# A spatial sum in three passes and a last stretch of queries in four chunks of 128, in a two-layer attention and gMLP kernel

## The chip, the cores and the metric

One core of one Trainium2 chip. The metric is device time in microseconds; the program is launched as a whole, and a time is the median of several executions. Executions of one kernel mostly agree within about 0.3%.

## The reference, cut to what matters

Two layers, each of an attention block A and a gated block B, over 2048 positions of 512 features. A has 32 query heads of 16 and one shared key and value head, so its softmax takes 32 x 2048 x 2048 exponentials a layer. B sums over positions, so it needs every position of its own layer before its last step.

```python
def _A_ref(x, wq, wk, wv, wo):            # S = 2048, D = 512, H = 32, Dh = 16, one k and v head
    scores = einsum('bhqd,bkd->bhqk', q, k) * Dh ** (-0.5)
    p = softmax(scores)
    o = einsum('bhqk,bkd->bhqd', p, v)
    return o.transpose(0, 2, 1, 3).reshape(B, S, H * Dh) @ wo

def _B_ref(x, w_in, w_sp, b_sp, w_out):   # F = 1792, Fh = 896
    z = gelu(x @ w_in)
    z1 = z[..., :Fh]
    z2 = layernorm(z[..., Fh:])
    g = einsum('ts,bsf->btf', w_sp, z2) + b_sp[None, :, None]     # the spatial sum
    return (z1 * g) @ w_out

x = A_x
for _ in range(2):                        # written out twice in the source
    x = x + _A_ref(layernorm(x), ...)
    x = x + _B_ref(layernorm(x), ...)
```

## The kernel before

The positions lie in 16 tiles of 128. Attention goes by chunks of queries; when a chunk is done its tiles go through the projection, the second layernorm, `w_in`, gelu and the norm of `z2`. The spatial sum over source tiles `s` goes in passes: tiles 0 to 7, tiles 8 to 13 (the early pass), and a closing that folds tiles 14 and 15 into the last step. `(8, 14, 4)` means tiles 8 to 13, once chunk 4 is through its gelu.

```python
self.chunks = [[256, 256, 512, 512, 256, 128, 128], [512, 512, 512, 256, 128, 128]]
self.passes = [[(0, 8, 2), (8, 14, 4)], [(0, 8, 1), (8, 14, 3)]]
self.gelus = [[(0, 1, 2), (3, 4), (5,), (6,)], [(0, 1), (2, 3), (4,), (5,)]]
self.s_fin = 14
...
def spatial(self, s0, s1, layer):
    acc = s0 > 0
    early = s1 == self.s_fin
    pr = PRE if early else PRP
    ...
    for tc in range(4):                       # 512 target positions each
        ... # load of the weights of this pass
        for f in range(NF):                   # 7 blocks of 128 features: 28 jobs a pass
            # one matmul of 512 columns per source tile, summed in PSUM
            ...
            def ev_fn(e, b, tc=tc, f=f):      # the eviction: one DVE add out of PSUM into gp
                dst = self.gp[:, tc, f, :]
                return e.tensor_tensor(dst, self.b32(b), dst if acc else self.bb[:, 512 * tc:512 * tc + 512], ALU.add)
            pl, (ev,) = sc.job(pieces, [dict(fn=ev_fn, ...)], deps, pr)
            if early:
                self.early_first.append(sc.first_op)
```

The exponentials are shared between ACT, which does most of them, and DVE, which makes a power of two by bit arithmetic. The DVE's share is decided by this rule, among others: while the first matmul of an early-pass job is ready and not placed, no DVE exponential starts.

```python
if EF and any(o.start is None and o.ready is not None and o.ready <= t for o in k.early_first):
    return None
```

The closing goes over eight groups of 256 target positions: matmuls of 256 columns over tiles 14 and 15, cast out of PSUM, add of `gp`, product with `z1`, then `w_out`.

```python
seq = [(i, f, s) for i, f in enumerate(fs) for s in range(s0, s1)]      # s0, s1 = s_fin, 16
...
ad = sc.op("dve", ... ALU.add ...)            # + gp, SBUF only
ev = sc.op("dve", ... ALU.mult ...)           # * z1, SBUF only
```

First, the order of the instructions on each engine is made ahead of the launch, by a list scheduler in the kernel's own Python. It reckons with durations of its own, of which two matter here. They decide only the plan: the order of the instructions and, with it, which of ACT and DVE takes some of the exponentials and casts.

```python
def d_psum(n):
    return n * 1.042e-3 + 0.066      # a DVE operation out of PSUM

def d_sb(n, rate):
    return n * rate + 0.066          # a DVE operation on SBUF
```

The scheduler, a list scheduler in the kernel's own Python that makes the order of the instructions ahead of the launch, fills some of PE's pauses with matmuls of a zero operand, which compute nothing. They show in the profile as busy PE time, on the line with `zero`.

The softmax here doesn't subtract the row's maximum and nothing guards it: scores larger than these inputs give would overflow.

Of the kernel before, what the change touches and what calls it, by code (L numbers as in the profile page):

```python
# [388 lines left out]
PRE = 1.6  # L389
PRP = 2.5  # L390
# [55 lines left out]
class Kern:  # L446
    def __init__(self, nc, A_x, A_wq, A_wk, A_wv, A_wo, B_x, B_w_in, B_w_sp, B_b_sp, B_w_out, out):
# [9 lines left out]
        self.chunks = [[256, 256, 512, 512, 256, 128, 128], [512, 512, 512, 256, 128, 128]]  # L457
        self.passes = [[(0, 8, 2), (8, 14, 4)], [(0, 8, 1), (8, 14, 3)]]
        self.gelus = [[(0, 1, 2), (3, 4), (5,), (6,)], [(0, 1), (2, 3), (4,), (5,)]]
        self.s_fin = 14  # L460
# [193 lines left out]
    def ln(self, tiles, deps_t, dst, dst_deps, pr, urgent=False, on_pe=False):  # L654
# [48 lines left out]
        return [ev]  # L703
# [149 lines left out]
    def finish_group(self, g, pv_last):  # L853
# [37 lines left out]
        if g.fin:  # L891
            tr = self.transpose(self.oTt[:, par, :].rearrange("p (i r) -> p i r", i=4), self.oT[:, par, :],
                                [ev, self.rd_read[par]], f"oq{par}", 0.5)
            self.oT_read[par] = tr
            m = sc.op("dve", lambda e: rc(e, None), 0.18, [tr], 0.6)
            for h in hs:
                m = sc.op("dve", lambda e, h=h: nm(h, e, None), d_psum(256 // len(hs)), [m] + onr, 0.5)
                self.norms.append(m)
            self.rd_read[par] = m
            if g.v == 1 and g.q.s0 + g.q.ns == 4:  # L900
                norms = self.norms
                self.norms = []
                self.project(g, norms)
            return
# [16 lines left out]
    def project(self, g, norms):  # L921
# [7 lines left out]
        for h in range((nq + 1) // 2):  # L929
# [16 lines left out]
            if g.fin > 1:  # L946
                for qt in qts:
                    o = self.transpose(self.onT[:, qt, :, :], self.on[:, qt, :], norms + list(self.onT_read), f"ot{qt}", 0.7)
                    self.on_read[qt] = [o]
                    evs.append(o)  # L950
                continue
# [6 lines left out]
            evs.append(ev)  # L958
# [18 lines left out]
    def mixer_chunk(self, g):  # L977
# [9 lines left out]
        for i in range(0, nt, 2):  # L987
            ts = T[i:i + 2]
            evs += self.ln(ts, lambda t: [self.x_op[t]], self.xnTB[:, i:i + len(ts), :, :], war, pr, last, g.fin == 1)
# [32 lines left out]
        elif g.ci == batch[-1] and len(batch) > 1 and g.ci > self.passes[g.layer][0][2]:  # L1022
# [44 lines left out]
    def mix_rest(self, g, last, pr, batch):  # L1067
# [27 lines left out]
        for ci, (zt, zn, v) in zip(batch, zs):  # L1095
# [8 lines left out]
            elif ci == batch[-1] and len(batch) > 1 and ci > self.passes[g.layer][0][2]:  # L1104
# [39 lines left out]
    early_first = []  # L1144
    gp_read = {}


    def spatial(self, s0, s1, layer):
# [3 lines left out]
        early = s1 == self.s_fin  # L1152
        pr = PRE if early else PRP
        z2f = self.z2n[:].rearrange("p t f -> p (t f)")
        wsl = self.wsT[:].rearrange("p s t -> p (s t)")
        if early:

            nf = self.NT - s1
            parts = [(z2f[:, 4096:4096 + 512 * nst], range(4, 4 + -(-(512 * (nst + 1)) // FH))), (wsl[:, 0:512 * nst], None)]
            self.held_f = range(0, 5)  # L1160
# [7 lines left out]
        for tc in range(4):  # L1168
            if early:
                w_, held = parts[tc % 2]  # L1170
                w_ = w_.rearrange("p (s t) -> p s t", s=nst)
                war = self.last_ws[0] if held is None else [o for t in held for o in self.z2_read[t]]
                ld = self.dma(lambda e, w_=w_, tc=tc: e.dma_start(w_, self.ws_dv[:, s0:s1, 512 * tc:512 * (tc + 1)]),
                              war + self.ws_st[s0:s1], f"wsp{tc % 2}", nst * 131072, 1.0)
# [14 lines left out]
            for f in range(NF):  # L1189
# [16 lines left out]
                def ev_fn(e, b, tc=tc, f=f):  # L1206
                    dst = self.gp[:, tc, f, :]
                    return e.tensor_tensor(dst, self.b32(b), dst if acc else self.bb[:, 512 * tc:512 * tc + 512], ALU.add)  # L1208
                pl, (ev,) = sc.job(pieces, [dict(
                    fn=ev_fn, dur=d_psum(512), prio=max(1.0, pr - 1.5),  # L1210
                    deps=list(self.gp_read[(tc, f)]) + ([self.gp_ops[(tc, f)]] if acc else []))], deps, pr)
                if early:
                    self.early_first.append(sc.first_op)
# [5 lines left out]
            if not early:  # L1219
                for i in (0, 1) if nsl == 1 else (sl,):  # L1220
                    self.last_ws[i] = [users[-1]]
            elif held is None:
                self.last_ws[0] = [users[-1]]


    def closing(self, layer):
# [6 lines left out]
        self.hT_read = [[o for o in self.dx_s.end], [o for o in self.dx_s.end]]  # L1233
        z1r = self.z1s[:].rearrange("p (k f t) -> p k f t", k=2, f=NF)
        zl = [list(self.z1s_free), list(self.z1s_free)]
        for tc in range(8):
            tg, to = tc // 2, 256 * (tc % 2)
# [630 lines left out]
```

## Time and profile before

| | before |
|---|---|
| time, median of 2 runs (range) | 1796.28 us (1794.82 to 1797.75) |
| last exponential of layer 0 | 851.2 us |
| gap to the first exponential of layer 1 | 37.0 us |
| exponentials of layer 1 | 850.6 us |
| tail from the last exponential to the end | 58.0 us |

Between the first and last exponential of a layer, ACT sets the pace. The gap and the tail have no exponentials, and there the closing and the keys of the next layer (or the output) set it. So a change can move four numbers: two long stretches and two short ones.

The next lines are busy times by stretch of the kernel before. The columns are the stretch in us, its length, then busy us (and instructions) of PE, PEld, DVE, ACT and POOL, then the granted clock, the DMA share and GB/s. The first two are the last 60 us of exponentials in each layer, then come the gap and the tail.

```profile
791.20:851.20 60.00, 58.57 (x419) 17.98 (x426) 22.21 (x36) 59.66 (x53) 0.81 (x2) 1.00 0.15 45
1678.80:1738.80 60.00, 58.68 (x419) 17.50 (x425) 28.35 (x43) 59.54 (x53) 0.81 (x2) 1.00 0.14 45
...
851.20:888.20 37.00, 36.08 (x258) 20.25 (x262) 33.10 (x88) 20.05 (x37) 4.31 (x8) 1.00 0.30 77
1738.80:1796.80 58.00, 56.39 (x346) 30.76 (x350) 46.69 (x112) 22.72 (x40) 1.91 (x4) 1.00 0.37 108
```

Read the third column of busy time (DVE) in the first two lines: 22 and 28 of 60 us. That is the idle time that the change is after. Then read the first (PE) in the last two: 36.1 of 37.0 and 56.4 of 58.0. PE is packed where the closing runs.

What PE does in the first 17 us of the tail is in its timeline (start, length, line, operands, count):

```profile
1740.66 0.39 PE L866 MATMUL ps_all<-ident,oT 128*128 128x128 bf16 x4
1740.89 1.03 PE L1196 MATMUL ps_all<-z2n 128*128 128x512 bf16 x4
1741.87 0.40 PE L937 MATMUL ps_all<-ident,on 128*128 128x128 bf16 x4
1742.11 1.03 PE L1196 MATMUL ps_all<-z2n 128*128 128x512 bf16 x4
1742.97 1.03 PE L966 MATMUL ps_all<-wo_r,onT 128*128 128x512 bf16 x4
1743.83 0.59 PE L1196 MATMUL ps_all<-z2n 128*128 128x512 bf16 x2
1744.27 3.18 PE L1196 MATMUL ps_all<-wsT,z2n 128*128 128x512 bf16 x13
...
1751.68 5.13 PE L1196 MATMUL ps_all<-wsT,z2n 128*128 128x512 bf16 x23
```

Lines 866, 937 and 966 are the chain of the last tile (transpose, transpose, projection). Each waits for another engine. Between them lie left-over jobs of the early pass (1196), which had been ready for long.

### The profile page before, as it was taken

Reading aid. Unit: us, or ns where it says so; the run is one execution under the profiler, and the core shown is the slowest. Engines: PE = TensorE matmul, PEld = TensorE weight load, DVE = VectorE, ACT = ScalarE, POOL = GpSimd, SP = SyncE. Lnnn points to the kernel's source line nnn. Section 1 sums busy time; section 2 is a strip of 40 time slices with the busy share of each in tenths; the row PEclk is TensorE's granted clock in tenths of the full one; section 3 lists DMA queues with packets and bytes.
Section 4 is the critical chain, followed back from the end, with each engine's and each line's share of the span. In section 5 each row is a group of like instructions: output and inputs, shape, how many; then the busy total and the mean of one; then the engine's idle time right before and its main releaser. Section 6 shows DMA issues by size and latency. Waiting matters only on the chain.

```text
span 1796.8 us, 29474 instructions
## 1 busy us (share of the span) xinstructions
PE 1563.1 (87%) x11691; PEld 464.7 (26%) x11773; DVE 1655.7 (92%) x2488; ACT 1722.0 (96%) x1557; POOL 56.4 (3%) x99
## 2 busy tenths in 40 slices
PE   8888888888989888999988888888888898898999
PEld 4222222212222222223532222222222222222235
DVE  8999999999999999973999999999999999999748
ACT  8999999999999999999689999999999999999983
POOL 1000000000000000000110000000000100000000
PEclk9999999999999999999999999999999999999999
DMA  4535100011010110311310001000110111203123
GB/s 148 124 77 135 54 18 4 7 30 24 10 47 27 30 48 13 77 37 54 87 36 10 4 7 19 18 7 4 30 24 13 45 30 30 51 7 77 35 82 114
DMA packets 155465, 76.14 MB, mean 42 GB/s; under 512 B 108480, under 2 KB 152128, under 8 KB 155328
## 3 DMA queue, kind: packets, MB, share of 16 engines
q1 hardware_dynamic: 153744, 74.08, 16.2%
q8 instruction: 94, 1.54, 0.4%
q14 instruction: 43, 0.35, 0.1%
q10 hardware_dynamic: 1584, 0.16, 0.1%
HBM read 31.49 MB, written 17.83 MB: 27 GB/s over the span
## 4 chain that ended last, share of the span: by engine, by line
ACT 50%; issue 20%; PE 18%; DVE 11%; POOL 1%; DMA 0%; ACTq 0%; DVEq 0%
ACT Pa L1471 49%; PE ps_all L1815 5%; PE ps_all L1196 5%; PE ps_all L1558 3%; DVE E L1667 1%; DVE st L1124 1%; PE ps_all L1286 1%; DVE st L660 1%; PE ps_all L1796 1%; DVE Pd L1698 1%; PE ps_all L998 1%; PE ps_all L1037 1%; DVE X L1291 1%; DVE E L1694 1%; DVE E L1268 1%
## 5 line engine op out<-in xcount | busy, mean ns | idle before, releaser
L1471 ACT ACTIVATE Pa<-ps_all 128x1536 bf16<-128x1536 f32 (+1 forms) x1424 | 1612.3, 1454 | 12.7 <-PE ps_all L1815 11.0
L1815 PE MATMUL ps_all<-qs,kT 32*128 32x512 bf16 x4096 | 561.0, 385 | 194.6 <-ACT Pa L1471 179.5
L1667 DVE TENSOR_SCALAR E<-ps_all 128x512 f32<-128x512 f32 x540 | 364.6, 682 | 28.4 <-PE ps_all L1815 25.7
L1796 PE MATMUL ps_all<-zero 128*128 128x512 bf16 x1065 | 331.2, 393 | 19.8 <-DVE mv L1126 6.2
L1815 PEld LDWEIGHTS ps_all<-qs,kT 32*128 32x128 bf16 x4096 | 138.6, 91 | 790.9 <-ACT Pa L1471 771.1
L1698 DVE SCALAR_TENSOR_TENSOR Pd<-E 128x1536 uint16<-128x1536 f32 x180 | 314.9, 1749 | 2.2
L1558 PE MATMUL ps_all<-Pa,V 128*32 128x512 bf16 x3556 | 316.5, 385 | 0.2 <-DVE oT L859 0.2
L1558 PE MATMUL ps_all<-Pd,V 128*32 128x512 bf16 x540 | 182.6, 385 | 0.0
L1696 DVE TENSOR_TENSOR E<-E 128x1536 f16<-128x1536 f16 x180 | 171.1, 951 | 2.2
L1694 DVE TENSOR_TENSOR E<-E 128x1536 f16<-128x1536 f16 x180 | 170.8, 949 | 2.4
L1692 DVE TENSOR_SCALAR E<-E 128x1536 f16<-128x1536 uint16 x180 | 171.2, 951 | 1.5
L1196 PE MATMUL ps_all<-wsT,z2n 128*128 128x512 bf16 x568 | 160.5, 382 | 9.2 <-issue 3.8
L1796 PEld LDWEIGHTS ps_all<-zero 128*128 128x128 bf16 x1065 | 81.4, 98 | 189.8 <-issue 129.8
L1695 DVE TENSOR_SCALAR E<-E 128x1536 f16<-128x1536 f16 x180 | 98.9, 550 | 1.0
L1558 PEld LDWEIGHTS ps_all<-Pa,V 128*32 128x32 bf16 x3556 | 62.0, 94 | 114.6 <-issue 108.5
L1208 DVE TENSOR_TENSOR gp<-ps_all,gp 128x512 f16<-128x512 f32 x56 | 38.4, 688 | 52.8 <-PE ps_all L1196 52.7
L1196 PEld LDWEIGHTS ps_all<-wsT,z2n 128*128 128x128 bf16 x616 | 44.0, 97 | 78.7 <-issue 43.7
L998 PE MATMUL ps_all<-w_in_r,xnTB 128*128 128x448 bf16 x256 | 63.5, 356 | 0.9 <-DVE z2n L1009 0.4
L1037 PE MATMUL ps_all<-xnTB,w_in_r 128*128 128x512 bf16 (+2 forms) x364 | 63.1, 299 | 0.6 <-DVE z2n L1009 0.3
L664 POOL TENSOR_SCALAR ve<-mv 128x2 f32<-128x2 f32 (+1 forms) x28 | 11.8, 421 | 1395.8 <-DVE mv L662 1395.7
L1265 ACT ACTIVATE E<-ps_all 128x512 f16<-128x512 f32 (+1 forms) x52 | 26.6, 538 | 29.3 <-PE ps_all L1253 28.6
L1286 PE MATMUL ps_all<-E 128*128 128x512 bf16 x214 | 52.6, 380 | 1.8 <-DVE kT L741 0.8
(87 smaller groups left out, 947.7 us busy)
## 6 DMA issues: line engine op xcount, KB each, us to landing
wsT_scratch<-gp SPq DMA_DIRECT2D x16, 512.0 KB, 3.6
wsT<-wsT_scratch SPq DMA_DIRECT2D x8, 1024.0 KB, 5.4
z1s<-z_scratch SPq DMA_DIRECT2D x16, 448.0 KB, 3.7
z_scratch<-z1s SPq DMA_DIRECT2D x4, 896.0 KB, 5.5
z2n<-wsT_scratch SPq DMA_DIRECT2D x4, 768.0 KB, 4.8
wsT<-wsT_scratch SPq DMA_DIRECT2D x4, 768.0 KB, 5.6
X<-in_A_x_dram SPq DMA_DIRECT2D x8, 256.0 KB, 5.8
z2n<-wsT_scratch SPq DMA_DIRECT2D x2, 1024.0 KB, 8.6
```

Of the source, the lines that this page charges most:

```text
L998: ins = e.matmul(self.b32(b)[:, 0:448], self.xnTB[:, i, kd, :], self.w_in_r[:, kd, FH + h * 448:FH + (h + 1) * 448], start=(kd == 0), stop ...
L1196: ins = e.matmul(self.b32(b), self.z2n[:, s, f * 128:(f + 1) * 128], w_[:, s - s0, :] if s - s0 < na or not spare else wsp[:, s - s0 - na, :],
L1471: return e.activation(k.Pa[:, base:base + n, :], k.b32(b0, n).rearrange("p (k q) -> p k q", k=n), ACTF.Exp, scale=SCALE)
L1558: ins = e.matmul(k.b32(u.grp.pvb)[32 * j:32 * j + 32, :], k.V[:, u.kt, :], b.slot, tile_position=(0, 32 * j), start=u.first, stop=u.last)
L1667: c = k.sc.op("dve", lambda e: e.tensor_scalar(k.ey[:, s, 512 * i:512 * (i + 1)], k.b32(j.bank.idx)[:, 0:512], E_LOG2, E_BIAS, op0=ALU.mul ...
L1692: o2 = sc.op("dve", lambda e: e.tensor_scalar(x, lo, E_X * 2.0 ** -16, E_X * E_A, op0=ALU.mult, op1=ALU.add), d_sb(n, 0.521e-3), self.ops ...
L1694: o3 = sc.op("dve", lambda e: e.tensor_tensor(w, x, x, ALU.mult), d_sb(n, 0.521e-3), [o2, self.wfree], pr)
L1695: o4 = sc.op("dve", lambda e: e.tensor_scalar(w, w, E_C, None, op0=ALU.add), d_sb(n, 0.26e-3), [o3], pr)
L1696: o5 = sc.op("dve", lambda e: e.tensor_tensor(w, w, x, ALU.mult), d_sb(n, 0.521e-3), [o4], pr)
L1698: o7 = sc.op("dve", lambda e: e.scalar_tensor_tensor(po.bitcast(U16), y, E_D, w, op0=ALU.add, op1=ALU.add), d_sb(n, 1.042e-3), [o5] + self ...
L1796: return e.matmul(k.b32(pvb if b is None else b.idx), k.zero[:], k.zero[:, None, :].to_broadcast([P, 4, P]), start=b is not None, stop=b i ...
L1815: return e.matmul(self.b32(bank), self.kT[32 * j:32 * j + 32, g.v, kt * 128:(kt + 1) * 128], self.qs[32 * j:32 * j + 32, g.q.slot, :], til ...
```

## The change

The intent: keep the early pass from holding up DVE's exponentials any longer, and let it come earlier, so that DVE takes more of them. For that, the last 512 queries become four chunks of 128, the second pass covers tiles 8 to 12, a short third pass takes tiles 13 and 14 as soon as they are there, and the closing is left with tile 15 alone. With `EFB = 0` only the third pass stops DVE's exponentials. Four of seven of the third pass's evictions are an ACT copy and a DVE add on SBUF in place of a DVE add out of PSUM.

```diff
-        self.chunks = [[256, 256, 512, 512, 256, 128, 128], [512, 512, 512, 256, 128, 128]]
-        self.passes = [[(0, 8, 2), (8, 14, 4)], [(0, 8, 1), (8, 14, 3)]]
-        self.gelus = [[(0, 1, 2), (3, 4), (5,), (6,)], [(0, 1), (2, 3), (4,), (5,)]]
-        self.s_fin = 14
+        self.chunks = [[256, 256, 512, 512, 128, 128, 128, 128], [512, 512, 512, 128, 128, 128, 128]]
+        self.passes = [[(0, 8, 2), (8, 13, 4), (13, 15, 6)], [(0, 8, 1), (8, 13, 3), (13, 15, 5)]]
+        self.gelus = [[(0, 1, 2), (3, 4), (5, 6), (7,)], [(0, 1), (2, 3), (4, 5), (6,)]]
+        self.s_fin = 15
 ...
-        early = s1 == self.s_fin
-        pr = PRE if early else PRP
+        early = acc
+        fin = s1 == self.s_fin
+        pr = (PRC if fin else PRE) if early else PRP
 ...
+            if fin:
+                pr = 2.0 + 2 * CLS * tc - CL0
 ...
-                pl, (ev,) = sc.job(pieces, [dict(
-                    fn=ev_fn, ...
-                if early:
+                if fin and f % 7 in CST:                       # CST = (0, 2, 4, 6)
+                    pl, (ev,) = sc.job(pieces, [dict(
+                        fn=lambda e, b, st=st: e.activation(st, self.b32(b), ACTF.Copy), eng="act", ...
+                    ev = sc.op("dve", lambda e, st=st, dst=self.gp[:, tc, f, :]: e.tensor_tensor(dst, st, dst, ALU.add), ...
+                else:
+                    pl, (ev,) = sc.job(pieces, [dict(
+                        fn=ev_fn, ...
+                if fin or early and EFB:                       # EFB = 0
                     self.early_first.append(sc.first_op)
 ...
         for tc in range(8):
+            pr = 2.0 + CLS * tc                                # closing, CLS = 0.1
```

Cut: where the weights of each pass are held, the staging buffers' bookkeeping, and tile 13 using the same transposes as the other small chunks.

## The prediction

> **What bounds the kernel now.** I read first the busy shares, then the forty slices, then the costliest groups, then the stretches of each layer's end, then the DVE's waits there, then the timeline of the last 60 us.
>
> ```profile
> PE 1563.1 (87%) x11691; PEld 464.7 (26%) x11773; DVE 1655.7 (92%) x2488; ACT 1722.0 (96%) x1557; POOL 56.4 (3%) x99
> ...
> DVE  8999999999999999973999999999999999999748
> ACT  8999999999999999999689999999999999999983
> ...
> L1471 ACT ACTIVATE Pa<-ps_all 128x1536 bf16<-128x1536 f32 (+1 forms) x1424 | 1612.3, 1454 | 12.7 <-PE ps_all L1815 11.0
> ```
>
> ACT does 3556 of the 4096 exponential blocks (128x512 each; 708 instructions of three and 716 of two) and is full nearly everywhere; five blocks leave it every 2.26 us, 0.452 us a block. DVE does the other 540 in batches of three. The DVE digit falls in two places only, the end of each layer, so the change is to be judged there. The stretches:
>
> ```profile
> 790.00:851.20 61.20, 59.77 (x425) 18.29 (x433) 23.41 (x38) 60.86 (x54) 0.81 (x2) 1.00 0.14 44
> 851.20:866.50 15.30, 15.19 (x106) 7.49 (x107) 11.78 (x25) 8.13 (x12) 1.91 (x4) 1.00 0.35 89
> 866.50:930.00 63.50, 60.24 (x482) 30.98 (x486) 61.00 (x160) 46.92 (x62) 8.33 (x16) 1.00 0.27 66
> ...
> 1684.00:1738.80 54.80, 53.48 (x389) 16.25 (x396) 23.25 (x38) 54.34 (x48) 0.81 (x2) 1.00 0.16 49
> 1738.80:1756.60 17.80, 17.70 (x117) 8.63 (x118) 13.16 (x27) 8.13 (x12) 1.91 (x4) 1.00 0.31 78
> 1756.60:1794.40 37.80, 36.58 (x221) 21.33 (x223) 33.52 (x85) 14.59 (x28) 0.00 (x0) 1.00 0.41 122
> ```
>
> The columns after the length are busy us of PE, PEld, DVE, ACT, POOL. For 55 to 61 us before the last exponential (at 851.2 and 1738.8) DVE is only 40% busy, ACT is full and PE shows 98%. Restricted to line 1667, the DVE's first step of an exponential, the same stretches show no instruction at all. The waits there say why DVE waits:
>
> ```profile
> DVE gp L1208 <- PE ps_all L1196: 25.9, 15, 2.5
> ```
>
> DVE waits for the early pass of the spatial sum (line 1196, tiles 8 to 13). The source has the other half: while the first matmul of an early-pass job is ready and not placed, no DVE exponential may begin. So DVE rests while ACT carries the exponentials alone, and PE fills every gap with the pass. After the last exponential PE is still packed: rest of the pass, the last tile's short chain, then the closing (lines 1253 and 1286). DVE is 89% busy in the last closing and 96% in layer 0's, which overlaps the keys of layer 1.
>
> ```profile
> 1756.64 3.00 PE L1253 MATMUL ps_all<-z2n 128*128 128x256 bf16 x26
> ...
> 1784.39 1.69 PE L1253 MATMUL ps_all<-z2n 128*128 128x256 bf16 x14
> ...
> 1793.05 1.34 DVE L1291 TENSOR_TENSOR X<-ps_all,X 128x512 bf16<-128x512 f32 x2 [0.92 <-PE ps_all L1286]
> ```
>
> **What the Trainium skill says.** "Perfetto Trace Analysis", section Identifying the Most-Contended Engine, says that matmul busy time does not tell how near TensorE is to its limit; so I count spacing. "TensorE: Matmul & The Clock Gate", section Back-to-back issue gap, gives 518 cycles for 512 columns and 262 for 256, 216 and 109 ns at 2.4 GHz, for isolated gaps, and a lower figure for sustained streams. This trace sides with the first: 23 spatial matmuls in a row show 5.13 us from the first's start to the last's end; with the modelled length of one taken off (0.38), that is 0.216 us each. "VectorE: DVE Perf Modes", section The perf-mode tier table, puts tensor_tensor with any PSUM operand at 1x and bf16 from SBUF at 2x. The trace agrees: an add out of PSUM takes 0.688 us (line 1208), the SBUF-only fp16 add of 512 (line 1268) 0.41 us alone and about 0.34 apart in a row. "ScalarE: Activation LUTs", section What ACT_TABLE_LOAD costs, says 1283 ns; the trace has 1283. The number of table switches doesn't change here.
>
> **The change, part by part.**
>
> 1. Chunks: 256 queries become 128 + 128. Exponentials, groups and query matmuls stay equal in total. Tile 12 finishes one 128-query chunk (about 50 us: 128/2048 of some 850 us a layer) before tile 13, so the middle gelu batch and the second pass come some 50 us earlier. The batch has five tiles for six. One tile is 0.95 + 0.93 = 1.88 us of ACT, taken out of the full part and put behind the last exponential, about -1.6 us per layer as DVE shares the gain. Tile 13 uses PE transposes rather than DMA ones, a few tenths of PE.
>
> 2. Second pass over tiles 8 to 12: 28 jobs x 5 = 140 matmuls for 168, 30 us of PE for 36. It no longer stops DVE's exponentials. The first pass, which runs that way, reached about 1.4 matmuls/us with its reload stalls (some 24 jobs of 8 in 140 us, 520 to 660). I take 3.5 us a job of five, 98 us in all, from about 750 and 1632. So it is nearly done at the last exponential, with some 2 jobs left; now 9 and 10 are left.
>
> 3. DVE exponentials in the freed time. They stop anyway about 25 us before the end, as the source stops 14 units of 4 blocks short (56 x 0.452 = 25 us). What remains idle before that is, by 5 us windows, about 20 us in layer 0 and 13.5 in layer 1. A batch costs 3 x 0.68 + 0.95 + 0.95 + 0.55 + 0.95 + 1.75 = 7.2 us, 2.4 a block. So 8 and 5.6 blocks leave ACT: about -3.3 and -2.3 us. More evictions inside the exponential part, some 15 x 0.688 = 10 us of DVE in both layers, cost 4 blocks: +1.8 us. Net of 1 to 3: 3.2 + 5.6 - 1.8 = 7 us off the two exponential parts.
>
> 4. Third pass over tiles 13 and 14, behind the last exponential: 56 matmuls x 0.216 = 12 us of PE. Of 28 evictions 12 go straight on DVE (8.3 us); 16 are ACT copies (0.54 to 0.60 us, 9 us of ACT) with an SBUF add on DVE (16 x 0.36 = 6 us). So 14 us of DVE per layer that did not exist, as two tiles were folded into the closing's own evictions.
>
> 5. Closing over one tile: 56 matmuls of 256 columns fewer, 56 x 0.109 = 6 us less PE. Its DVE work stays.
>
> 6. The tail of layer 1, from the last exponential. PE before: some 54 left-over matmuls 11.6, the last tile's chain 4.8, closing 8 x 4.5 = 36, so 52 of the 55.6 us. PE after: 2 jobs 2.2, third pass 12, chain 4.8, closing 30, so 49, with a hole of some 4 us before tiles 13 and 14 are normalised. DVE before: 13.2 + 33.5 = 46.7. DVE after: 46.7 - 8 x 0.688 + 14.3 + 2 (statistics and normalising of one more tile) = 57.5; perhaps 2.8 of it, four casts of the closing, can go to ACT. The tail turns from PE-bound to DVE-bound, and becomes 57 to 58 us, about +2. In layer 0, where DVE was full already, the same extra 10 us meets key building: I take +2 too, as ACT can take casts and key copies.
>
> Sum: -7 + 4 = -3 us from the rows. Parameters such as the ACT/DVE split look tuned, so I lean to less cost in the tails: -6, 1790 us.
>
> **Rivals.** (a) The extra DVE work of the tails is fully exposed, 8 to 10 us each, while the exponentials gain 7: +10, 1806. For it: DVE at 96% in layer 0's closing. Against it: ACT is busy only 14.6 of 37.8 us in layer 1's closing. (b) The second pass is starved by the DVE exponentials, for both need the same two side banks, and half of it remains at the end: 14 jobs x 1.08 = 15 us of PE, in part hidden in the 4 us hole; then +5 per tail, about 1800. For it: the first pass made no eviction from 660 to 718. Against it: the second has a higher priority and shorter jobs. (c) PE time is what counts, and moving the pass into the middle, where filler matmuls take about a tenth of PE (line 1796, 0 to 3 us in each 10 us), frees more than I count: the 7 or 8 jobs no longer left over, and the 6 us off each closing, come off each tail, and the third pass hides in the last tile's chain. Then -8 per layer with the exponentials' 7: about 1775. For it: PE above 96% in all these stretches. (d) DVE exponentials do not resume, as mixer work of two more small chunks keeps DVE busy: 1796.
>
> **Range and chances.** The parts are each within 8 us and of opposite sign; (c) and (a) make the ends. 1790 us, with 1776 to 1804 to hold it 8 times in 10. A change of 2% is 36 us, more than all idle DVE time in these stretches could give if turned into exponentials: 69 us / 2.4 x 0.452 = 13 us. So faster by over 2% 0.02, within 2% 0.96, slower by over 2% 0.02.
>
> **What would show it.** Line 1667 with instructions in the last 60 us before the last exponential, about 14 more in all, and DVE near 80% there: step 3. The second pass nearly finished at the last exponential: step 2. The last exponential of layer 0 3 to 5 us earlier, that of layer 1 6 to 9 us earlier less whatever layer 0's transition lost. Third-pass matmuls starting 7 to 9 us after it. DVE above 95% from there to the end, with a tail of 57 to 58 us: step 6. If the tail is shorter than 54 us, PE was the bound and DVE had room (c); if over 61, (a) or (b), told apart by the left-over jobs. A lower granted clock or a long DMA wait on the third pass's weights would be outside all of it.

## More of the kernel before

`w_sp` is 0.01 x 0.05 x normal, so single terms of the spatial sum are tiny in the output. Experiments that falsify a few of them can still be reported correct.

## The result, and the profile after

The changed kernel takes 1806.58 us (median of 2 runs, 1806.33 to 1806.83), 10 us more than before. The ratio is 1.0052, with a 95% interval of 1.0028 to 1.0077. A ratio is the mean time of one kernel's fast runs over that of the other's in the same rounds, so it is not quite the ratio of the medians quoted. By the 2% rule this is "same", as predicted, but the time lies outside the predicted range, and on the other side of the time before.

| us, from the traces | before | after | difference |
|---|---|---|---|
| last exponential of layer 0 | 851.2 | 848.3 | -2.9 |
| gap | 37.0 | 42.3 | +5.3 |
| exponentials of layer 1 | 850.6 | 855.3 | +4.7 |
| tail | 58.0 | 59.2 | +1.2 |
| span | 1796.8 | 1805.0 | +8.2 |

The page of the changed kernel, its busy line and two of its groups (DVE's first step of an exponential, and its eviction of the spatial sum):

```profile
PE 1568.8 (87%) x11812; PEld 460.9 (26%) x11812; DVE 1689.1 (94%) x2568; ACT 1738.2 (96%) x1591; POOL 62.0 (3%) x107
...
L1700 DVE TENSOR_SCALAR E<-ps_all 128x512 f32<-128x512 f32 x545 | 368.9, 682 | 30.1 <-PE ps_all L1848 27.6
...
L1222 DVE TENSOR_TENSOR gp<-ps_all,gp 128x512 f16<-128x512 f32 x80 | 54.3, 684 | 30.7 <-PE ps_all L1210 29.9
```

DVE is 33 us busier and does 545 exponential blocks in place of 540. Most of its new time goes elsewhere: 80 evictions for 56, and the 32 SBUF adds of the staged ones. The same stretches as before, last 60 us of exponentials, then gap and tail:

```profile
788.30:848.30 60.00, 57.95 (x429) 17.76 (x422) 39.46 (x63) 59.78 (x54) 0.79 (x2) 1.00 0.17 55
1685.90:1745.90 60.00, 57.65 (x433) 17.78 (x434) 37.42 (x59) 59.71 (x54) 0.79 (x2) 1.00 0.15 47
...
848.30:890.50 42.20, 39.59 (x256) 19.29 (x255) 39.77 (x106) 27.81 (x51) 5.36 (x10) 1.00 0.36 95
1745.90:1805.00 59.10, 54.02 (x303) 25.78 (x299) 52.83 (x134) 30.70 (x58) 2.73 (x6) 1.00 0.42 119
```

The first two lines say that the release works: DVE goes from 22.2 to 39.5 and from 28.4 to 37.4 us of 60. Its first exponential step (line 1700) shows 6 times in each of these windows, where there was none. The gap has 6.7 us more of DVE and 3.5 more of PE. The tail has 6.1 more of DVE and 2.4 less of PE. But PE's time in the tail is not all work; its timeline shows what stands in the place of the left-over jobs:

```profile
1747.09 0.40 PE L871 MATMUL ps_all<-ident,oT 128*128 128x128 bf16 x4 [0.80 <-DVE oT L864]
1747.33 0.81 PE L1829 MATMUL ps_all<-zero 128*128 128x512 bf16 x3
1748.30 0.40 PE L942 MATMUL ps_all<-ident,on 128*128 128x128 bf16 x4 [0.17 <-DVE on L891]
...
1749.23 0.61 PE L1829 MATMUL ps_all<-zero 128*128 128x512 bf16 x2 [0.31 <-ACT z2n L1088]
1751.02 1.04 PE L971 MATMUL ps_all<-wo_r,onT 128*128 128x512 bf16 x4 [1.19 <-DVE onT L958]
1751.89 1.34 PE L1829 MATMUL ps_all<-zero 128*128 128x512 bf16 x4
1753.26 2.33 PE L1210 MATMUL ps_all<-z2n 128*128 128x512 bf16 x10
```

The chain of the last tile is the same (871, 942, 971), but between its steps PE now runs zero matmuls or waits. The first useful spatial matmul (1210, the third pass) comes at 1753.26, some 7.4 us after the last exponential, when tiles 13 and 14 are normalised. I call the time without a useful matmul under way a hole. Counted from the trace it is 9.7 us in this tail for 3.8 before, and 4.5 us in this gap for 0.9.

### The profile page after: what moved, and what is told of

Its sections match the earlier page's. It is cut to its first block, busy times and chain, and to the rows that moved or that the text cites. A ratio compares the mean times of both kernels' runs of the same rounds, so it can differ in the third digit from the quotient of the medians.

```text
span 1805.0 us, 29778 instructions
## 1 busy us (share of the span) xinstructions
PE 1568.8 (87%) x11812; PEld 460.9 (26%) x11812; DVE 1689.1 (94%) x2568; ACT 1738.2 (96%) x1591; POOL 62.0 (3%) x107
## 4 chain that ended last, share of the span: by engine, by line
ACT 55%; issue 20%; PE 14%; DVE 11%; DMA 1%; POOL 0%; ACTq 0%
ACT Pa L1504 52%; PE ps_all L1848 4%; PE ps_all L1210 3%; PE ps_all L1591 3%; DVE st L665 1%; PE ps_all L1829 1%; ACT z2n L1088 1%; DVE X L1324 1%; DVE E L1304 1%; DVE E L1700 1%; DVE gp L1222 1%; DVE E L1301 1%; PE ps_all L1042 1%; PE ps_all L1003 1%; DVE xn L680 1%
## 5 line engine op out<-in xcount | busy, mean ns | idle before, releaser
L1700 DVE TENSOR_SCALAR E<-ps_all 128x512 f32<-128x512 f32 x545 | 368.9, 682 | 30.1 <-PE ps_all L1848 27.6
L1829 PE MATMUL ps_all<-zero 128*128 128x512 bf16 x1040 | 320.5, 390 | 18.2 <-DVE mv L1131 6.1
L1731 DVE SCALAR_TENSOR_TENSOR Pd<-E 128x1536 uint16<-128x1536 f32 (+1 forms) x184 | 318.1, 1729 | 2.3
L1210 PE MATMUL ps_all<-wsT,z2n 128*128 128x512 bf16 x644 | 177.0, 382 | 4.3 <-DVE gp L1222 2.0
L1725 DVE TENSOR_SCALAR E<-E 128x1536 f16<-128x1536 uint16 (+1 forms) x184 | 173.2, 941 | 1.9
L1729 DVE TENSOR_TENSOR E<-E 128x1536 f16<-128x1536 f16 (+1 forms) x184 | 172.8, 939 | 2.2
L1727 DVE TENSOR_TENSOR E<-E 128x1536 f16<-128x1536 f16 (+1 forms) x184 | 172.8, 939 | 2.1
L1728 DVE TENSOR_SCALAR E<-E 128x1536 f16<-128x1536 f16 (+1 forms) x184 | 99.8, 543 | 1.1
L1222 DVE TENSOR_TENSOR gp<-ps_all,gp 128x512 f16<-128x512 f32 x80 | 54.3, 684 | 30.7 <-PE ps_all L1210 29.9
L1042 PE MATMUL ps_all<-xnTB,w_in_r 128*128 128x128 bf16 (+2 forms) x420 | 64.1, 281 | 1.2 <-DVE E L1700 0.4
L1210 PE MATMUL ps_all<-z2n 128*128 128x512 bf16 x196 | 53.2, 382 | 2.1 <-DVE gp L1222 1.1
```

Source lines behind the costliest of these rows:

```text
L1042: ins = e.matmul(self.b32(b)[:, (f - f0) * n:(f - f0 + 1) * n], self.w_in_r[:, kd, f * 128:(f + 1) * 128], self.xnTB[:, 0:n // 128, kd, :] ...
L1210: ins = e.matmul(self.b32(b), self.z2n[:, s, f * 128:(f + 1) * 128], w_[:, s - s0, :] if s - s0 < na or not spare else wsp[:, s - s0 - na, :],
L1700: c = k.sc.op("dve", lambda e: e.tensor_scalar(k.ey[:, s, 512 * i:512 * (i + 1)], k.b32(j.bank.idx)[:, 0:512], E_LOG2, E_BIAS, op0=ALU.mul ...
L1725: o2 = sc.op("dve", lambda e: e.tensor_scalar(x, lo, E_X * 2.0 ** -16, E_X * E_A, op0=ALU.mult, op1=ALU.add), d_sb(n, 0.521e-3), self.ops ...
L1727: o3 = sc.op("dve", lambda e: e.tensor_tensor(w, x, x, ALU.mult), d_sb(n, 0.521e-3), [o2, self.wfree], pr)
L1728: o4 = sc.op("dve", lambda e: e.tensor_scalar(w, w, E_C, None, op0=ALU.add), d_sb(n, 0.26e-3), [o3], pr)
```

## The experiments

Eighteen kernels ran, three rounds each. One table gathers those of the three orders.

### One part of the third pass thinned: e1, e2, e5

The first suspicion was rival (a) of the prediction: the DVE work of the third pass. e1 keeps every instruction in its place and narrows the third pass's evictions (ACT copy, staging add, PSUM add) from 512 to 8 columns. The planned durations are untouched, so the order stays.

```diff
-e.activation(st, self.b32(b), ACTF.Copy)
+e.activation(st[:, 0:8], self.b32(b)[:, 0:8], ACTF.Copy)
-e.tensor_tensor(dst, st, dst, ALU.add)
+e.tensor_tensor(dst[:, 0:8], st[:, 0:8], dst[:, 0:8], ALU.add)
+if fin:
+    return e.tensor_tensor(dst[:, 0:8], self.b32(b)[:, 0:8], dst[:, 0:8], ALU.add)
```

> The changed kernel with its instruction order untouched; only the third pass's 28 evictions per layer (16 ACT copies with their DVE adds, 12 DVE adds out of PSUM) are narrowed from 512 to 8 columns. The result is wrong on purpose. Theory A (the third pass's evictions are exposed DVE work: 13 to 14 us per layer behind the last exponential): the gap between the last exponential of layer 0 and the first of layer 1 (42.3 us after, 37.0 before) and the tail behind the last exponential of layer 1 (59.2 us) each shrink by 3 to 6 us; total 1794 to 1800. Rival B (PE is what counts there, the 56 extra matmuls): gap and tail move by less than 1.5 us each, total 1804 to 1807.

Measured: 1804.18 us, ratio 1.0043 [1.0028, 1.0058], reported correct although the sum is falsified. The gap is 42.1 us, the tail 58.6. Its stretches (gap, tail):

```profile
847.30:889.40 42.10, 39.58 (x256) 19.48 (x255) 32.26 (x108) 22.64 (x52) 5.34 (x10) 1.00 0.36 95
1744.00:1802.60 58.60, 53.91 (x303) 26.15 (x299) 43.88 (x134) 24.74 (x58) 2.72 (x6) 1.00 0.42 120
```

DVE loses 7.5 and 9.0 us of work in these stretches, ACT 5 and 6, and the stretches lose 0.2 and 0.5. So with the order fixed, the length of the evictions on DVE and ACT does not set the gap or the tail. What that leaves is PE, the chain, and the number of jobs.

e2 narrows the third pass's matmuls instead, from 512 to 64 columns, and e5 does both.

```diff
-ins = e.matmul(self.b32(b), self.z2n[...], w_[:, s - s0, :] ...
+ins = e.matmul(self.b32(b)[:, 0:64] if fin else self.b32(b), self.z2n[...], w_[:, s - s0, 0:64] if fin else ...
```

> The changed kernel with its order untouched; only the third pass's 56 matmuls per layer are narrowed from 512 to 64 columns, their evictions stay whole. Wrong on purpose. Theory A (evictions): gap and tail move by less than 2 us each, total 1803 to 1807. Rival B (PE): 56 matmuls lose some 8 us of PE per layer, gap and tail shrink by 4 us or more each, total below 1799.

> The changed kernel with its order untouched; the third pass's matmuls narrowed to 64 columns and its evictions to 8, both at once (wrong on purpose). The two runs that thinned one of them moved gap and tail by less than 2.2 us. If the two engines bind together, so that relieving one leaves the other: gap 36 to 39 us (42.3 in the changed kernel), tail 53 to 56 (59.2), total 1793 to 1799. If the fixed order and the number of instructions bind, not their width: gap and tail within 2 us of the changed kernel's, 1801 to 1807.

Measured: e2 1811.84 us, ratio 1.0081 [1.0065, 1.0096], wrong result; e5 1802.86 us, 1.0037 [1.0022, 1.0052]. Less work on PE did not make e2 faster: its gap is 44.4 us and its tail 60.0, outside both of my bands, though its interval overlaps with that of the changed kernel (1.0028 to 1.0077). In e5 the gap is 43.0 and the tail 57.4, as my second idea had it. The granted clock shows why these two can't decide: in the first 15.3 us behind layer 0's last exponential it was 1.00 in e1, 0.89 in e2 and 0.81 in e5. With less to do PE was granted less (the last section takes this up). Whether the lower clock cost time isn't shown: e5, granted least, was the fastest of the three. I take e2 and e5 as inconclusive on PE's part.

### The four chunks alone, then with the release: e3, e4

e3 is the kernel before with the four chunks of 128 and nothing else: the early pass goes over tiles 8 to 13 as before and still stops DVE's exponentials, and the closing keeps tiles 14 and 15. e4 is e3 with the release.

```diff
-[256, 256, 512, 512, 256, 128, 128], [512, 512, 512, 256, 128, 128]
+[256, 256, 512, 512, 128, 128, 128, 128], [512, 512, 512, 128, 128, 128, 128]
-[(0, 8, 2), (8, 14, 4)], [(0, 8, 1), (8, 14, 3)]
+[(0, 8, 2), (8, 14, 5)], [(0, 8, 1), (8, 14, 4)]
-[(0, 1, 2), (3, 4), (5,), (6,)], [(0, 1), (2, 3), (4,), (5,)]
+[(0, 1, 2), (3, 4, 5), (6,), (7,)], [(0, 1), (2, 3, 4), (5,), (6,)]
 # e4 only:
-EF = 1
+EF = 0
```

> The kernel before with one part of the change: the last 512 queries as four chunks of 128. Two passes as before (tiles 0-7, 8-13, the second still holding back DVE exponentials), closing over tiles 14 and 15. If the third pass is what costs: 1793 to 1799, gap 36 to 39 us, tail 57 to 59 us. If the small chunks cost (more chains, one more batch of small evictions): 1802 or more with the exponentials of both layers ending later.

> The four chunks and the released second pass (it no longer holds back DVE exponentials), but no third pass: tiles 0-7, 8-13, closing over 14 and 15. If the release helps as the prediction said and the third pass takes it away again: 1784 to 1793, faster than the kernel before, with at least 6 DVE exponentials more per layer than its 270 and the last exponential of layer 0 at 845 to 849 us. If the release is worth nothing: within 2 us of the four chunks alone.

Measured: e3 1796.03 us, ratio 0.9998 [0.9983, 1.0013]; e4 1800.31 us, 1.0022 [1.0006, 1.0039]. The time of e3 is what I expected if the third pass costs; e4 missed its band of 1784 to 1793. In e3 fewer jobs are left over (4 and 7 PSUM evictions behind the last exponentials, for 8 and 10), the gap is 35.0 and the tail 55.0, but DVE does 10 blocks fewer in all. In e4 DVE does 548 blocks, layer 0's exponentials end 5.0 us before e3's, and 10 and 10 jobs are left over, which goes with 4.3 us more in the gap and 1.9 in the tail. So it looks as if a block that DVE takes early is in part paid by a spatial job that runs late.

### The release undone, and layer 1 alone: e6, e7

e6 is the changed kernel with the second pass stopping DVE's exponentials again (`EFB = 1`). e7 gives layer 0 its old chunks, passes and closing and leaves layer 1 changed.

```diff
 # e6
-EFB = 0
+EFB = 1
 # e7
-self.chunks = [[256, 256, 512, 512, 128, 128, 128, 128], [512, 512, 512, 128, 128, 128, 128]]
+self.chunks = [[256, 256, 512, 512, 256, 128, 128], [512, 512, 512, 128, 128, 128, 128]]
 ... (passes, gelus and s_fin of layer 0 likewise)
```

> The changed kernel with one part undone: the second pass again holds back DVE exponentials while one of its jobs waits. If the release is a gain that the third pass hides: slower, 1815 to 1828, with some 10 DVE exponentials fewer per layer than 276 and 269. If the release is itself the loss (banks and PE time taken by DVE exponentials delay the pass): 1795 to 1803.

> Layer 0 with the old chunks and passes, layer 1 with the new ones. If each layer pays its own price: layer 0's last exponential near 851 and the gap near 37 us as before, the exponentials of layer 1 some 5 us longer than the 850.6 us before, tail 59 us, total 1801 to 1805. If layer 1's loss came only from what layer 0's transition handed on, or from the luck of the order: exponentials of layer 1 within 2 us of 850.6, total 1795 to 1800.

Measured: e6 1824.86 us, ratio 1.0161 [1.0146, 1.0176]; e7 1803.45 us, 1.0051 [1.0033, 1.0069]. Without the release the changed kernel loses 18 us, and its DVE does 511 blocks. So the release is a large gain inside the changed kernel, and something else outweighs it. (Its trace has half the clock for 23.9 and 20.5 us up to the layers' last exponentials, but ACT is over 99% busy in them, so that isn't the loss.) In e7 the gap is 37.0, as before; layer 1 alone loses 3.6 us in its exponentials and 2.7 in its tail.

### Another order of the same work: e8 to e12

In the changed kernel part of the loss of layer 1's exponentials came in the middle of the layer, where both kernels hold the same work: between its 1000th and 1200th exponential block (of 2048) it fell back by 3 us against the kernel before. (In e7 the loss came in the last fifth of the layer.) That pointed to the order. e8 is e4, with the scheduler's two constants moved by 1 or 2 ns. The work is the same; the list scheduler, which compares reckoned times, puts it in another order. A few instructions change their engine with it: DVE does 550 exponential blocks for 548. I picked this pair of constants because, among those tried, the scheduler's own plan for it came out short.

```diff
-return n * 1.042e-3 + 0.066      # d_psum
+return n * 1.042e-3 + 0.064
-return n * rate + 0.066          # d_sb
+return n * rate + 0.065
```

> The four chunks and the released second pass without a third pass, as in the fourth run, with the durations that the kernel's own list scheduler assumes for a DVE read of PSUM and of SBUF 2 ns and 1 ns shorter: the same work in another order. If the fourth run lost to the kernel before by the luck of its order, an order of the same work can be faster than both kernels: 1783 to 1791. If it is the parts themselves: within 3 us of the fourth run's 1800.

Measured: 1787.09 us, ratio 0.9956 [0.9940, 0.9973]. It beats both kernels, and it beats e4, which has the same work, by 13 us. Gap and tail of e8:

```profile
844.80:881.30 36.50, 35.67 (x256) 20.07 (x259) 32.58 (x87) 20.06 (x37) 4.46 (x8) 1.00 0.30 79
1731.10:1785.20 54.10, 51.14 (x321) 28.31 (x323) 43.91 (x108) 22.22 (x39) 1.89 (x4) 1.00 0.40 116
```

Then one pick can't be compared with another pick, so I ran the kernel before and the changed kernel in two other orders each: order B with the SBUF constant at 0.067 alone, order C with e8's constants. Order A is the kernel as given.

> The kernel before with nothing changed but the two constants by which its own list scheduler reckons an eviction and an SBUF operation of DVE (0.064 and 0.065 in place of 0.066), the same shift that took the released chunks from 1800 to 1787. Same instructions, other order. If that gain was a better order for anyone, this kernel gains 10 us too: about 1786. If the order is only a draw (theory: luck of some 4 us either way, and the kernel before was the pick of its own neighbours), it lands at 1797 to 1803.

> The changed kernel with the same shift of the two constants, nothing else. Systematic loss (rival): the changed kernel stays 8 to 12 us behind the kernel before, at 1804 to 1808. Luck of the order (theory): it moves by several us, anywhere from 1798 to 1812. At 1795 or less my view that the third pass costs anything would be wrong.

> The changed kernel with the scheduler's constant for an SBUF operation of DVE 0.067 for 0.066: same work, a second other order. Theory: 1798 to 1812, not within 1 us of 1806.6. Rival (the loss is systematic): 1804 to 1808.

> The kernel before with the same constant at 0.067: same work, other order. Theory (its order was a lucky one): slower than 1796.3, 1798 to 1803. Rival (the order hardly matters): within 2 us of 1796.3.

Measured: before 1803.1 (C; ratio 1.0041 [1.0026, 1.0056]) and 1807.69 (B; 1.0060 [1.0045, 1.0075]); changed 1813.5 (C; 1.0097 [1.0080, 1.0114]) and 1812.57 (B; 1.0089 [1.0074, 1.0105]). All ratios are to the kernel before in order A. The constants of e8 are not good for any kernel: they cost the kernel before 7 us. The order moves one kernel by 7 to 13 us, more than I had expected (all four lie above my bands for the theory, by 0.1 to 4.7 us). And both ideas hold at once: the kernel before has the luckiest of its three orders, and the changed kernel is behind in every order, by 10.3 us in A, 4.9 in B and 10.4 in C.

### The table filled: e13, e14, e15

The same two orders for the chunks alone and the released chunks.

> The released chunks (four chunks of 128, second pass out of DVE's way, no third pass) with the scheduler's constant for an SBUF operation of DVE 0.067: the third of three orders in which the kernel before (1796, 1803, 1808) and the changed one (1807, 1814, 1813) have run. Known so far of this variant: 1800 and 1787. Theory (the third pass costs, the rest gains or is even): below 1803, so that its mean over three orders stands at least 5 us under that of the kernel before. Rival (1787 was one lucky draw): 1803 to 1810.

> Four chunks alone, second pass still stopping DVE's exponentials, in the order that gave 1803 for the kernel before and 1787 for the released chunks. If the release carries the gain: 1800 to 1806. If the chunks carry it: 1790 or less.

> Four chunks alone, constant at 0.067. If the chunks are neutral: 1802 to 1810, as the kernel before in that order (1808). If they carry a gain: below 1798.

Measured: e13 1798.93 (1.0019 [1.0002, 1.0035]), e14 1803.59 (1.0041 [1.0026, 1.0056]), e15 1801.53 (1.0028 [1.0013, 1.0043]). e13 and e14 fell in the bands of the theory, e15 between its two.

| us, medians | order A | order B | order C | mean |
|---|---|---|---|---|
| before | 1796.3 | 1807.7 (e12) | 1803.1 (e9) | 1802.4 |
| four chunks | 1796.0 (e3) | 1801.5 (e15) | 1803.6 (e14) | 1800.4 |
| four chunks, released | 1800.3 (e4) | 1798.9 (e13) | 1787.1 (e8) | 1795.4 |
| the same with the third pass: the changed kernel | 1806.6 | 1812.6 (e11) | 1813.5 (e10) | 1810.9 |

Three orders are few, and their scatter is some 6 us either way, so only the large differences count. The third pass costs 6.3, 13.6 and 26.4 us in the three orders, 15 in the mean. This is the price of the whole step from the released chunks to the changed kernel, and with the third pass come a shorter second pass and gelu batch, tile 13's gelu behind the last exponential in place of before it, other places for the weights and new priorities of the closing (`CLS`). No run separates these. The released chunks gain 7 in the mean over the kernel before, though in order A they lose. The stages, as means over the three orders, with PE's holes:

| us | before | chunks | released | changed |
|---|---|---|---|---|
| last exponential of layer 0 | 848.3 | 852.7 | 846.9 | 851.2 |
| gap (of it hole) | 37.9 (0.9) | 35.3 (5.8) | 38.4 (0.7) | 42.7 (6.0) |
| exponentials of layer 1 | 856.0 | 855.0 | 852.8 | 855.5 |
| tail (of it hole) | 57.9 (3.6) | 55.0 (6.4) | 55.0 (4.0) | 59.6 (10.3) |

The stretches of the chunks alone are also a floor. With 2 to 7 jobs left over the gap stays at 35.0 to 35.9 and the tail at 55.0, and the holes grow instead. So up to some 8 left-over jobs are nearly free (e8, with 8 and 6, has 36.5 and 54.1): they fill the last tile's chain.

Part of what I call order is the granted clock. Each trace of the twelve kernels of the table has one to five stretches, 3.4 to 17.1 us long, in which the clock is 0.5, and they lie mostly in other places from order to order. In layer 1 of e4 one starts at 1403.0, just behind a batch of gelus (columns as before, then ACT's timeline):

```profile
1402.00:1410.00 8.00, 6.08 (x29) 1.27 (x33) 6.50 (x10) 4.43 (x5) 0.00 (x0) 0.57 0.01 3
...
1404.59 2.53 ACT L1471 ACTIVATE Pa<-ps_all 128x1536 bf16<-128x1536 f32 x2 [2.12 <-PE ps_all L1815]
1408.46 2.52 ACT L1471 ACTIVATE Pa<-ps_all 128x1536 bf16<-128x1536 f32 x2 [1.34 <-PE ps_all L1815]
```

ACT waits 3.9 us for PE there, with a third wait of 0.40; at the same work, with the full clock, it waits 0.4 us in the kernel before and 0.8 in e8. So some 3 of the 13 us between e4 and e8 stand in this place. Over all executions the time of one kernel falls by about 0.8 us for each 0.001 of mean granted clock (my fit within kernels). Put to a clock of 0.996 by this fit, the four means of the table (of medians) become 1802.0, 1800.5, 1796.5 and 1809.2: their ranking stays. Why the clock halves where it does was not tested.

### The third pass without the chunks: e16

The old chunks, second pass over tiles 8 to 13 and released, third pass over tile 14 alone, closing over tile 15.

```diff
-[(0, 8, 2), (8, 13, 4), (13, 15, 6)], [(0, 8, 1), (8, 13, 3), (13, 15, 5)]
+[(0, 8, 2), (8, 14, 4), (14, 15, 5)], [(0, 8, 1), (8, 14, 3), (14, 15, 4)]
 # chunks, gelus and their conditions as in the kernel before
```

> The old chunks (256 and two of 128) with a third pass over tile 14 alone and the closing over tile 15 alone, second pass over tiles 8 to 13 released, as in the changed kernel. The same 28 extra evictions and adds per layer as in the changed kernel, but only 28 matmuls in the third pass. Theory (the third pass's number of instructions in the layer's end costs, and not the chunks): the stretch between the layers' exponentials is 41 to 44 us for 37 and the whole 1803 to 1815. Rival (the four chunks cost): 37 to 40 us, 1795 to 1800.

Measured: 1821.29 us, ratio 1.0137 [1.0122, 1.0152]; gap 51.5, tail 64.4. Its gap and tail:

```profile
846.90:898.40 51.50, 48.66 (x292) 21.75 (x291) 45.33 (x113) 27.84 (x53) 4.40 (x8) 1.00 0.30 86
1754.10:1818.40 64.30, 60.44 (x332) 27.87 (x330) 55.38 (x136) 30.98 (x60) 1.91 (x4) 1.00 0.36 104
```

The kernel is slow without the chunks too, so the rival, that the chunks cost, falls. It came worse than I expected: 24 and 22 evictions straight from PSUM stand behind the last exponentials. 12 are the third pass's (its other 16 go by ACT), so 12 and 10 jobs of the second pass stand there too. What the third pass costs by itself can't be read from this run, as the old chunks with the release and without a third pass never ran.

### The third pass without its wait: e17, e18

The third pass reads tiles 11 and 12, which are normalised long before, in place of 13 and 14. The result is wrong (it was still reported correct, since these terms are tiny). The jobs, evictions and adds stay. e17 is in order A, e18 in order B.

```diff
-self.z2n[:, s, f * 128:(f + 1) * 128]
+self.z2n[:, s - 2 if fin else s, f * 128:(f + 1) * 128]
-[self.z2_op[s] for s in range(s0, s1)]
+[self.z2_op[s] for s in (range(s0 - 2, s1 - 2) if fin else range(s0, s1))]
```

> The changed kernel with its third pass reading tiles 11 and 12, which are normalised long before, in place of 13 and 14 (a wrong result on purpose): the same instructions in the same number, only their wait for tiles 13 and 14 is gone. In the three orders of the changed kernel PE's hole (time without a useful matmul) behind the exponentials is 4.5 to 7.5 us in the gap and 9.7 to 10.7 us in the tail, against 0.6 to 0.9 and 3.2 to 5.1 in the kernel before and the released chunks. Theory (the wait makes the holes, and the holes the loss): gap below 2 us of hole and at most 40 us long, tail below 6 of hole and at most 56 long, the whole 1793 to 1800. Rival (the number of extra jobs, evictions and adds is what costs): gap 41 us or more, whole 1803 or more.

> The same with the scheduler's constant for an SBUF operation of DVE 0.067, the order in which the changed kernel took 1812.6. Theory: holes as in the run before, whole at least 8 us under 1812.6, so at most 1804.6. Rival: 1808 or more.

Measured: e17 1807.61 us, ratio 1.0053 [1.0025, 1.0081]; e18 1808.62 us, 1.0060 [1.0035, 1.0085]. The gap shrank from 42.2 to 38.5 (hole 4.5 to 1.8) and from 43.0 to 40.2 (hole 7.5 to 3.8); the tail from 59.2 to 57.8 and from 60.2 to 59.2. PE at the start of e17's gap:

```profile
851.62 2.75 PE L1210 MATMUL ps_all<-z2n 128*128 128x512 bf16 x11
854.59 0.40 PE L942 MATMUL ps_all<-ident,on 128*128 128x128 bf16 x4 [0.22 <-DVE on L891]
854.82 1.04 PE L1210 MATMUL ps_all<-wsT,z2n 128*128 128x512 bf16 x4
855.70 1.03 PE L971 MATMUL ps_all<-wo_r,onT 128*128 128x512 bf16 x4
856.56 2.32 PE L1210 MATMUL ps_all<-wsT,z2n 128*128 128x512 bf16 x10
```

The third pass (1210) now stands between the steps of the chain, as the left-over jobs did before. In e17 it starts 1.9 and 3.0 us after the last exponentials, where the changed kernel starts it 7.8 and 7.4 us after them; so it was the wait for the tiles that held it back, and not a late load of its weights. So the wait for tiles 13 and 14 makes about 3 to 4 us of the gap's excess. But the whole gained nothing in order A, where layer 1's exponentials took 3.5 us longer (by the table loads of ACT, 2.6 us of it is a second split of the gelus, told of below), and 4 us in order B. My theory for the whole missed in both runs. The rival, that the extra jobs cost by themselves, was met in both by the whole; its gap of 41 us or more in e17 was not. The wait shapes the gap; it is not most of the 15 us.

## Why the prediction was right or wrong

The verdict within 2% was right and the argument for it held: all the idle time of these stretches is small against 36 us. The time was wrong: -6 us predicted, +10 measured. The terms of its sum beside the two traces, and beside the means of three orders:

| us | predicted | traces, order A | means |
|---|---|---|---|
| exponentials of both layers (steps 1 to 3) | -7 | +1.8 | +2.4 |
| gap (steps 4 to 6) | +2 | +5.3 | +4.8 |
| tail (steps 4 to 6) | +2 | +1.2 | +1.7 |

So the sum of -3 missed by 11 us, and 9 of them lie in the exponentials. (The lean from -3 to -6 came on top. Two slips in the sum are small: at 0.452 us a block, 8 and 5.6 blocks are 3.6 and 2.5 us, not 3.3 and 2.3. And its tail ends at 1794.4, so its 57 to 58 us are 59.4 to 60.4 in the measure of this document.)

**Steps 1 to 3, the exponentials: the term that failed most.** The mechanism is there: the chunks with the release gain 4.6 us in these stretches in the mean of three orders (and 7 in all), and DVE does 547 to 550 blocks for 540; I had counted on some 10 more, net. What failed is the assumption that this gain would survive the rest of the change. In the changed kernel only 542 to 545 blocks are left in the three orders, and the 7 us are gone: the last exponential of layer 1 came 7.1 us later than before (5.3 of it from the gap), where I had named 6 to 9 us earlier less the gap's loss. The next paragraph accounts for a part; what step 1's -1.6 us a layer came to, no run separates. DVE rose to 66 and 62% in the last 60 us, not to 80%: it still waits for the second pass (line 1222 on line 1210) there, 15.4 us in layer 1's last 60.

```profile
DVE gp L1222 <- PE ps_all L1210: 15.4, 9, 4.7
```

**"The number of table switches doesn't change": wrong.** The loads of ACT's function tables are 15, 15 and 17 in the three changed kernels for 13 in the kernel before. The gelus of tiles 8 to 12 run as one batch in two parts (first `z2`, line 1088, then `z1`, line 1084), and in four of the six layers of the three changed kernels an exponential slipped between the parts. The timeline of ACT in layer 0 (order A):

```profile
732.69 1.28 ACT L1088 ACT_TABLE_LOAD   x1
733.98 4.03 ACT L1088 ACTIVATE z2n<-z2n 128x3584 bf16<-128x3584 bf16 x2
738.03 1.28 ACT L1504 ACT_TABLE_LOAD   x1
739.32 1.02 ACT L1504 ACTIVATE Pa<-ps_all 128x1024 bf16<-128x1024 f32 x1
740.37 1.28 ACT L1084 ACT_TABLE_LOAD   x1
741.66 3.19 ACT L1084 ACTIVATE z1s<-z1s 128x3584 bf16<-128x3584 bf16 x1
```

One exponential of 1.02 us costs two loads of 1.28. None of the nine kernels without the third pass in the table has this split, and each of its four cases costs at least 2 x 1.28 = 2.6 us, so 1.7 us a layer in the mean. With the blocks that DVE lost against the released chunks (3.0 in layer 0 and 1.7 in layer 1, at 0.452 us) this comes to 3.1 and 2.5 us. The step from the released chunks to the changed kernel made these stretches 4.3 and 2.7 us longer. This is an account from the traces, and in the mean alone (in layer 0 of order B, 6.2 us longer, there is no split); no run took the split away. Nor does it always come with the third pass: e7 has the same batch in layer 1, and no split.

**Steps 4 to 6, the ends of the layers: the gap mis-sized, the tail right by luck.** I put +2 on each. Against the kernel before in the same orders the gap grew by 4.8 and the tail by 1.7; against the released chunks the gap costs 4.3 us and the tail 4.5, in the mean. The prediction's work counts were good: it had 49 us of PE left in the tail, and 49.5 us of useful matmuls were there; third-pass matmuls were to start 7 to 9 us after the last exponential, and started at 7.4. What failed is what I made of them. I said that the tail turns DVE-bound, with a PE hole of "some 4 us". DVE was busy 52.8 of 59.1 us, and e1 took 9 us of its work away for a gain of 0.5, so it is not the bound in that order. The hole was 9.7 us, 6.0 more than before, and against the 5 us of useful matmuls saved this gives the +1. In the gap I had assumed no hole at all; it was 4.5. In the kernel before, the left-over jobs of the early pass were not a cost to be removed: they filled the last tile's chain. The third pass takes about their number of matmuls (56 for 56 in the tail) but can't start before tiles 13 and 14 are normalised. e17 and e18 show that this wait makes most of the gap's excess over the released chunks (without it the gap shrinks by 3.8 us in order A, where the excess is 3.0, and by 2.8 of 3.6 in B), and a smaller part of the tail's (1.4 of 2.3 and 1.0 of 6.0).

**The starting point.** I took the kernel before's 1796 as a fair draw. Its own two other orders took 1808 and 1803, mostly in layer 1's exponentials (850.6 us for 858.3 and 859.2). In the mean of the three orders the change costs layer 1's exponentials nothing (856.0 before, 855.5 after), although the one pair of traces shows +4.7 there; it makes layer 0's 2.9 us later (848.3 and 851.2), where the pair shows -2.9. So of the measured +10, about 8.5 is the change in the mean of three orders, and the rest is not a step at all: in any one order a change that replaces the schedule is redrawn by several us. My range of 28 us was about as wide as that scatter; its centre was what was off.

**The rivals.** (a) named 1806 and it came out at 1806.6, by luck: it had 7 us gained in the exponentials and 8 to 10 lost at each end, where some 2 were lost in the exponentials, 5 in the gap and 1 to 2 in the tail; and its cause, exposed DVE work, isn't what e1 shows. (b), half of the second pass left over, did not happen: in order A 2 second-pass evictions were left in layer 0 and none in layer 1, by count of the evictions straight from PSUM less the third pass's 12. (c), that PE time is what counts, failed at the floor: e14 with 2 and 3 jobs left over has a gap no shorter than e3 with 4 and 7. (d), that DVE exponentials don't resume, is refuted by line 1700's 6 instructions in each of the last 60 us.

**What stays open.** How the 15 us of the step to the third pass divide between its jobs' own work, its waits, the split gelus, the granted clock and what else came with it. Of the thinned runs e1 and e5 took 2 to 4 us away, which is within the noise, and e2 added 5; the removed wait took 4 or none, and the split is worth up to 5.2 by count. Each was measured in one or two orders only, and each new version is again a redraw.

## What to carry to other kernels

Work that is ready and left over behind a critical chain may be filling the chain's pauses; before you move it away, count the time without useful work on that engine, and ask whether the replacement can start as early. When an instruction order comes from a list scheduler, compare versions in several orders of each (a nanosecond on a planning constant is enough to redraw it): here the same work differed by up to 13 us in time, more than the effect under study. And look at which part of a change carries the gain: four chunks with the release, without the third pass, took 1787.09 us in the best of three orders, faster than both kernels in theirs (and 1795.4 for 1802.4 and 1810.9 in the means).

## What the Trainium skill lacked or had wrong

- "ScalarE: Activation LUTs", section What ACT_TABLE_LOAD costs: it adds some 1380 ns of drain to the 1283 ns of a load, 2.66 us for each switch. Here the load of 1.28 us at 738.03 is followed by the exponential at 739.32, and the load of 1.28 us at 732.69 by the gelu at 733.98, with no drain visible. Two exponentials in a row overlap by 0.35 us in this trace (median) and don't overlap across a load, so a switch cost at most 1.28 + 0.35 + 0.03 = 1.66 us.
- "TensorE: Matmul & The Clock Gate", section What's actually happening: it says that the clock gate is set by how busy PE has recently been, and the thinned kernels agree: 1.00, 0.89 and 0.81 granted in the same 15 us of e1, e2 and e5. What no page that I found says, is what follows for such experiments: a run with narrowed matmuls changes the clock along with the work, so it doesn't isolate PE's part. That the lower clock costs time, these runs don't show: e2 took 1811.84 us and e5, granted less, 1802.86, for 1806.58.
- No page that I found has the scatter between orders of the same work: 1796 to 1808 us for the kernel before and 1787 to 1800 for the released chunks, in three orders each.
